# Both halves of the weighted values ahead of the two multiplies that read them, in a fused attention and feed-forward kernel

## The chip, the cores and the metric

The kernel runs on one core of one Trainium2 chip. The metric is the time of one execution on the device in microseconds (us), and the median over several executions is quoted. A profiled execution also gives a span, from the first to the last instruction, which is about 1.8 us shorter than that time; slots and waits below are read in the span. PE is TensorE (PEld its weight loads), DVE is VectorE, ACT is ScalarE, POOL is GpSimd. The granted clock is the share of TensorE's full clock that the profile shows as granted: 1.00 is full, 0.50 half. The chain is the work that ended last, followed back from the last instruction through what each step waited for.

## The reference, cut to what matters

```python
# q, k, v: (8, 12, 448, 64)
scores = q @ k.T / sqrt(64)
e = exp(scores - m)
attn = e / (sum(e) + exp(-m) + 1e-09)      # softmax "off by one"
x = (attn @ v)  -> (3584, 768)
h = x @ w_in                               # 768 x 2048
g = h * tanh(softplus(h))                  # mish
out = g @ w_out                            # 2048 x 768
```

The kernel leaves out the maximum: it computes exp(scores) and divides by sum + 1, as logarithm with bias 1 and exponential with scale -1.

## The kernel before

Four heads make a group; there are 24 groups, three to a batch. The weighted values of a group are two halves of 32 columns per head. Four matmuls lie side by side in the array (one per head), four times over, so 16 matmuls make a half. Each half is written to its own 512 columns of one tile of 2 x 512; such a part is called a bank below:

```python
    def sums(g):
        den = m_pool.tile([128, 512], FP32, tag="m", name="den_ps")
        side_by_side(den, g, lambda c, t: ones[0:P, :])
        rc = work.tile([128, S], FP32, tag="rc", name="rc")
        nc.scalar.activation(out=rc, in_=den[:, 0:S], func=AF.Ln, bias=1.0)
        nc.scalar.activation(out=rc, in_=rc, func=AF.Exp, scale=-1.0)
        rc_t[g] = rc

    def attend(g):
        ...
        av = s_pool.tile([128, 2, 512], FP32, tag="s", name="av_ps")
        ...
        for s in range(2):
            side_by_side(av[:, s], g, lambda c, t: vs[:, c, t, s])
            nc.vector.tensor_mul(x_t[b][:, gi, s, :], av[:, s, 0:S], rc)
```

`s_pool` has three buffers of two banks, and the score tiles use them too: `scores` takes a buffer, two matmuls fill it, and one exponential on ScalarE empties it. `m_pool` has two buffers of one bank. After the first groups, each slot of the program runs like this, with matmuls of the feed-forward part (`after_a`, `after_b`, `after_c`) between the scores of the next two pairs of heads, and with mish work on ScalarE in 14 of the slots:

```python
    def group_slot(u, after_a, after_b, after_c, gates_of=None):
        prepare(2 * u)
        sums(u - 1)
        if gates_of is not None:
            mish(*gates_of)
        attend(u - 1)
        if 2 * u < J:
            scores(2 * u, (0, 1))
        run(after_a)
        ...
        scores(2 * u, (2, 3))
        scores(2 * u + 1, (0,))
        run(after_b)
        ...
        scores(2 * u + 1, (1, 2, 3))
        run(after_c)
```

The softmax here doesn't subtract the row's maximum and nothing guards it: scores larger than these inputs give would overflow.

## Time and profile before

| | before |
|---|---|
| time, median of 3 runs | 470.77 us (469.59 to 471.0) |
| span of the profiled run, granted clock | 467.7 us, 1.00 |
| TensorE busy | 427.6 us, 91% |
| ScalarE busy | 285.3 us, 61% |
| VectorE busy | 139.4 us, 30% |
| TensorE waits for the multiply between the halves | 27.4 us in 24 pieces |

TensorE is the engine to watch, since it is busy nearly all the time and makes most of the chain that ended last. What counts is therefore the time in which it stands still, and what it stands still for. The lines are in the prediction.

### The profile page before, as it was taken

The page shows a single profiled execution, that of the slowest core. Times are in us where ns is not written, and L with a number is a line of the kernel's source. Part 1 is how long each engine was busy: PE and PEld are TensorE (multiplying, and loading weights), DVE is VectorE, ACT ScalarE, POOL GpSimd, SP SyncE. Part 2 cuts the span into 40 slices and gives each one's busy share as a digit, 9 for nine tenths or more (in the row PEclk, how much of TensorE's full clock was granted, in tenths as well). Part 3 has the DMA queues.
Part 4 walks back from the last instruction along what each step waited for, and adds up shares of the span by engine and source line. Part 5 has one row for each costly group of instructions (what it writes and reads, how often), then busy time and mean ns, then how long its engine had stood idle before and what let it go on. Part 6 is the DMA issues. An engine that isn't in the chain of part 4 may idle for free.

```text
span 467.7 us, 8046 instructions
## 1 busy us (share of the span) xinstructions
PE 427.6 (91%) x3424; PEld 215.8 (46%) x3424; DVE 139.4 (30%) x232; ACT 285.3 (61%) x346; POOL 87.0 (19%) x144
## 2 busy tenths in 40 slices
PE   7898987998999999999999999999999999999996
PEld 2334443444544445444445445444445444545563
DVE  1224342442224421344223431244223432110021
ACT  3785588777934977458864769349773679342200
POOL 6454131210122211130112311131021100000000
PEclk9999999999999999999999999999999999999999
DMA  9999996330669326770486435590455301210222
GB/s 197 202 202 204 209 180 158 81 80 24 149 167 203 81 67 146 180 170 1 114 205 156 136 80 125 143 229 0 114 142 152 85 2 34 69 35 0 69 68 67
DMA packets 77700, 55.21 MB, mean 118 GB/s; under 512 B 36576, under 2 KB 74208, under 8 KB 77664
## 3 DMA queue, kind: packets, MB, share of 16 engines
q1 hardware_dynamic: 64288, 44.32, 38.6%
q0 software_dynamic: 13216, 10.19, 14.1%
q8 instruction: 26, 0.43, 0.4%
q10 hardware_dynamic: 160, 0.20, 0.1%
q14 instruction: 10, 0.08, 0.1%
HBM read 45.61 MB, written 11.01 MB: 121 GB/s over the span
## 4 chain that ended last, share of the span: by engine, by line
PE 78%; ACT 13%; DVE 3%; DMA 3%; issue 1%; POOL 1%; DVEq 0%; POOLq 0%
PE o_ps L261 31%; PE h_ps L207 29%; PE s_ps L153 8%; PE av_ps L176 4%; PE den_ps L176 4%; ACT e L160 4%; ACT rc L189 3%; DVE xT L201 3%; ACT rc L188 3%; DMA kq<-in_q_dram 3%; ACT gm L238 2%; ACT L239 1%; ACT L235 1%; PE tr_ps L136 1%; DMA out_dram<-o_sb 0%
## 5 line engine op out<-in xcount | busy, mean ns | idle before, releaser
L160 ACT ACTIVATE e<-s_ps 112x896 bf16<-112x896 f32 x192 | 162.7, 917 | 82.7 <-PE s_ps L153 81.9
L207 PE MATMUL h_ps<-xT,w_in_sb 128*128 128x448 bf16 x768 | 152.5, 353 | 0.0
L261 PE MATMUL o_ps<-w_out_sb,gm 128*128 128x384 bf16 x768 | 131.3, 326 | 0.0
L207 PEld LDWEIGHTS <-w_in_sb 128*128 128x128 bf16 x768 | 72.4, 98 | 74.5 <-issue 10.9
L261 PEld LDWEIGHTS <-gm 128*128 128x128 bf16 x768 | 72.9, 98 | 55.1 <-issue 8.6
L215 DVE COPY h_sb<-h_ps 128x448 f32<-128x448 f32 x112 | 70.0, 625 | 85.8 <-PE h_ps L207 85.8
L279 DVE COPY o_sb<-o_ps 128x384 f32<-128x384 f32 x54 | 30.1, 558 | 150.1 <-PE o_ps L261 136.7
L176 PE MATMUL av_ps<-e,v_b 112*32 112x448 bf16 x768 | 45.3, 353 | 27.4 <-DVE xT L201 27.4
L115 POOL CAST kq<-k_f 112x512 bf16<-112x512 f32 x36 | 22.1, 615 | 201.2 <-DMA k_f<-in_k_dram 139.7
L153 PE MATMUL s_ps<-qk 64*112 64x448 bf16 x384 | 55.5, 373 | 4.0 <-ACT e L160 3.3
L201 DVE TENSOR_TENSOR xT<-av_ps,rc 128x448 bf16<-128x448 f32 x48 | 30.0, 625 | 60.5 <-ACT rc L189 35.5
L188 ACT ACTIVATE rc<-den_ps 128x448 f32<-128x448 f32 x24 | 13.1, 547 | 50.9 <-PE den_ps L176 50.9
L176 PEld LDWEIGHTS <-v_b 112*32 112x32 bf16 x768 | 20.9, 96 | 46.7 <-issue 34.1
L238 ACT ACTIVATE gm<-h_sb 128x1536 bf16<-128x1536 f32 x28 | 39.8, 1467 | 0.0
L153 PEld LDWEIGHTS <-qk 64*112 64x112 bf16 x384 | 20.8, 126 | 36.1 <-issue 29.1
L119 POOL CAST v_b<-v_f 112x512 bf16<-112x512 f32 x36 | 22.1, 614 | 54.3 <-PE av_ps L176 49.5
L176 PE MATMUL den_ps<-e,ones 112*32 112x448 bf16 x384 | 23.3, 355 | 0.4 <-ACT e L160 0.2
L115 POOL CAST kq<-q_f 112x512 bf16<-112x512 f32 x36 | 22.1, 614 | 3.5 <-DMA q_f<-in_q_dram 2.8
L219 ACT ACTIVATE gm<-h_ps 128x384 bf16<-128x384 f32 x16 | 7.9, 491 | 22.6 <-PE h_ps L207 22.6
L261 PE MATMUL o_ps<-w_out_sb,gt 128*128 128x384 bf16 x128 | 21.5, 326 | 0.0
L239 ACT ACT_TABLE_LOAD x14 | 18.0, 1283 | 0.3
L235 ACT ACT_TABLE_LOAD x14 | 18.0, 1283 | 0.2
(29 smaller groups left out, 109.9 us busy)
## 6 DMA issues: line engine op xcount, KB each, us to landing
k_f<-in_k_dram SPq DMA_DIRECT2D x37, 224.0 KB, 3.6
q_f<-in_q_dram SPq DMA_DIRECT2D x37, 224.0 KB, 3.8
v_f<-in_v_dram SPq DMA_DIRECT2D x36, 224.0 KB, 4.0
w_in_sb<-in_moe_w_in_dram POOLq DMA_DIRECT2D x8, 384.0 KB, 12.1
w_out_sb<-in_moe_w_out_dram POOLq DMA_DIRECT2D x4, 768.0 KB, 16.0
out_dram<-o_sb SPq DMA_DIRECT2D x8, 336.0 KB, 3.2
out_dram<-o_sb SPq DMA_DIRECT2D x8, 288.0 KB, 2.8
out_dram<-o_sb SPq DMA_DIRECT2D x8, 240.0 KB, 2.7
```

The lines of the kernel that those rows point to most:

```text
L115: nc.gpsimd.tensor_copy(out=mb[:, i].rearrange("p t h d -> p h t d"), in_=loaded.pop((j, name)).rearrange("p h (t d) -> p h t d", d=D),)
L153: nc.tensor.matmul(sp[0:P, h, 0:S], lhsT=qk[r, 0, t * P : (t + 1) * P], rhs=qk[r, 1, :], start=True, stop=True,)
L160: nc.scalar.activation(out=e_t[j][:, t], in_=sp[0:P, :, 0:S], func=AF.Exp, scale=SCALE)
L176: nc.tensor.matmul(ps[c * 32 : c * 32 + 32, 0:S], lhsT=weights(c, t), rhs=e_t[2 * g + c // 2][:, t, c % 2, :], start=(t == 0), stop=(t == ...
L188: nc.scalar.activation(out=rc, in_=den[:, 0:S], func=AF.Ln, bias=1.0)
L201: nc.vector.tensor_mul(x_t[b][:, gi, s, :], av[:, s, 0:S], rc)
L207: nc.tensor.matmul(hp[:, 0:S], lhsT=w_in_sb[:, dm // 2, dm % 2, ff * 128 : (ff + 1) * 128], rhs=x_t[b][:, dm // 2, dm % 2, :], start=(dm = ...
L215: nc.vector.tensor_copy(out=h_sb[:, ff, :], in_=hp[:, 0:S])
L235: nc.scalar.activation(out=gt[:, f, o : o + TAIL], in_=h_sb[:, f, MAIN:S], func=AF.Mish)
L238: nc.scalar.activation(out=gm[:, f, :], in_=h_sb[:, f, 0:MAIN], func=AF.Mish)
L261: nc.tensor.matmul(op[:, 0:HALF], lhsT=lhs, rhs=w_out_sb[:, ff, n * HALF : (n + 1) * HALF], start=(ff == 0), stop=(ff == FF_T - 1),)
L279: nc.vector.tensor_copy(out=o_sb[:, cols], in_=op[:, 0:HALF])
```

## The change

The intent is that the second half should not wait for the multiply of the first. They share a tile, and in the program's order the write of the second half comes after a read of that tile.

```diff
         for s in range(2):
             side_by_side(av[:, s], g, lambda c, t: vs[:, c, t, s])
+        for s in range(2):
             nc.vector.tensor_mul(x_t[b][:, gi, s, :], av[:, s, 0:S], rc)
```

## The prediction

> **What bounds the kernel now.** I read the page first (busy shares, then the chain that ended last), then the waits of TensorE, then the timeline of one slot, and last, for every slot, when each score tile starts and when the buffer that it reuses comes free.
>
> ```profile
> PE 427.6 (91%) x3424; PEld 215.8 (46%) x3424; DVE 139.4 (30%) x232; ACT 285.3 (61%) x346; POOL 87.0 (19%) x144
> PE 78%; ACT 13%; DVE 3%; DMA 3%; issue 1%; POOL 1%; DVEq 0%; POOLq 0%
> L176 PE MATMUL av_ps<-e,v_b 112*32 112x448 bf16 x768 | 45.3, 353 | 27.4 <-DVE xT L201 27.4
> L239 ACT ACT_TABLE_LOAD x14 | 18.0, 1283 | 0.3
> PE av_ps L176 <- DVE xT L201: 27.4, 24, 1.2
> PE s_ps L153 <- ACT e L160: 3.3, 4, 2.1
> ```
>
> TensorE (PE) bounds it: 91% busy, 78% of the chain. Its one large wait is the one that the change is about: 27.4 us in 24 pieces, one for each group of four heads, up to 1.2 us each. All other waits of TensorE together are about 8 us: 3.3 us for exponentials (second line of waits) and the rest nearly all in the first 17 us. The 13% of ScalarE (ACT) and 3% of VectorE (DVE) in the chain are mostly this detour: sums, logarithm, exponential, multiply, second half. The table load's count tells that 14 of the 24 slots also do mish work on ScalarE; this will matter. Here is one such slot, TensorE's lines first:
>
> ```profile
> 222.96 0.94 PE L176 MATMUL den_ps<-e,ones 112*32 112x448 bf16 x16
> 223.72 0.93 PE L176 MATMUL av_ps<-e,v_b 112*32 112x448 bf16 x16
> 225.81 0.94 PE L176 MATMUL av_ps<-e,v_b 112*32 112x448 bf16 x16 [1.16 <-DVE xT L201]
> 226.68 0.59 PE L153 MATMUL s_ps<-qk 64*112 64x448 bf16 x4
> 227.20 5.37 PE L261 MATMUL o_ps<-w_out_sb,gm 128*128 128x384 bf16 x32
> ...
> 224.53 0.58 ACT L189 ACTIVATE rc<-rc 128x448 f32<-128x448 f32 x1
> 225.12 1.28 ACT L235 ACT_TABLE_LOAD   x1
> 226.41 0.63 ACT L235 ACTIVATE gt<-h_sb 128x512 bf16<-128x512 f32 x1
> 226.95 2.84 ACT L238 ACTIVATE gm<-h_sb 128x1536 bf16<-128x1536 f32 x2
> 229.81 1.28 ACT L239 ACT_TABLE_LOAD   x1
> ...
> 225.13 0.62 DVE L201 TENSOR_TENSOR xT<-av_ps,rc 128x448 bf16<-128x448 f32 x1 [1.51 <-ACT rc L189]
> 226.80 0.62 DVE L201 TENSOR_TENSOR xT<-av_ps,rc 128x448 bf16<-128x448 f32 x1 [1.04 <-PE av_ps L176]
> ```
>
> The first half of the weighted values runs at 223.72. Its multiply needs the reciprocal (ready at 225.11) and ends at 225.75; the second half, into the other bank of the same tile, starts only then, at 225.81. It needs neither. The next lines are the last exponential and the last score tile that end the slack of this slot, and the same two of a slot of another kind (36 us later) and of a third without mish:
>
> ```profile
> 231.92 0.91 ACT L160 ACTIVATE e<-s_ps 112x896 bf16<-112x896 f32 x1
> 232.93 0.35 PE L153 MATMUL s_ps<-qk 64*112 64x448 bf16 x2
> ...
> 268.54 0.91 ACT L160 ACTIVATE e<-s_ps 112x896 bf16<-112x896 f32 x1
> 270.02 0.35 PE L153 MATMUL s_ps<-qk 64*112 64x448 bf16 x2
> ...
> 244.31 0.91 ACT L160 ACTIVATE e<-s_ps 112x896 bf16<-112x896 f32 x1
> 249.30 0.35 PE L153 MATMUL s_ps<-qk 64*112 64x448 bf16 x2
> ```
>
> The score tiles and the weighted values' tile share three buffers. The score tile in the second line reuses the buffer that the exponential in the first line frees: free at 232.83, used at 232.93, a slack of 0.10 us. In the other two kinds it is 0.57 and 4.08 us.
>
> **What the Trainium skill says.** "PSUM — Partial Sum Buffer", in its summary of rules for kernel authors, asks for reads of PSUM during matmuls to go to a different bank, guarded by bank. The two halves are in different banks, so nothing of that kind asks for the wait; it comes from the shared tile. The trace agrees only that the wait exists. "Perfetto Trace Analysis", Matmuls, says that independent matmul groups should rotate through different banks so that an evacuation overlaps the next group; here the evacuation doesn't overlap. "TensorE: Matmul & The Clock Gate", Packing small matmuls, gives starts of about 4 ns apart for packed tiles; the trace has 3 to 4 ns within four matmuls and about 0.19 us from four to four. "ScalarE: Activation LUTs", What ACT_TABLE_LOAD costs, gives 1283 ns and a drain of 1380 ns more; the trace shows 1283 ns, but mish starts 0.01 us after the load, so I count no drain.
>
> **The change part by part.** No instruction is added or removed. The built kernel's lists show two moves: the second half's first matmul no longer waits for VectorE, and the first multiply waits for all 32 matmuls of its tile, the second for nothing.
>
> *Saved on TensorE, per slot.* Start to start, sums to first half is 223.72 - 222.96 = 0.76 us, for the same 16 matmuls and a change of tile. First to second half is 2.09 us. It should become 0.76, so 1.33 us is freed; a little more than the idle 1.16 us, since the pipeline's fill goes too. For 24 slots that is 32 us at most.
>
> *The multiplies.* The second half will start at 224.48 and end at 225.42. The first multiply moves from 225.13 to about 225.46, the second ends at about 226.72 in place of 227.42. All later readers get their data sooner, and VectorE (30% busy) has room.
>
> *What stays of it.* ScalarE's chain in a slot hangs on the end of the sums (223.93), which doesn't move: logarithm, exponential, table load, mish, table load, then exponentials of the slot's first two score tiles, ending at 232.83. So in a mish slot TensorE comes to its fifth score tile 1.33 us earlier, but the buffer doesn't. The slot keeps min(1.33, slack - 0.05), 0.05 being the least distance from exponential to matmul in the trace. By the same two columns for all slots:
> - 6 slots without mish (groups 3, 8, 11, 14, 17, 20), where the exponentials follow their scores at once and move with them, and the last one (23, no scores follow): 7 x 1.33 = 9.3 us.
> - Group 2: its last sums already wait for an exponential, and the second half could start at 37.03 in place of 38.33: 1.3 us.
> - 5 mish slots (9, 12, 15, 18, 21) with slack 0.57 to 0.58: 5 x 0.53 = 2.6 us.
> - 6 mish slots (7, 10, 13, 16, 19, 22) with slack 0.10: 6 x 0.05 = 0.3 us.
> - 3 mish slots (4, 5, 6) where TensorE waits for the exponential already (the 3.3 us above): 0.
> - Groups 0 and 1, before mish begins: ScalarE sets the pace there, idle 1.27 and 1.22 us until the first scores after the second half. In group 0 the halves are 1.75 apart: 1.75 - 0.76 = 1.0 us. In group 1 the scores come 1.9 us earlier, counting the first, so 0.9 us more. Together 1.9 us.
>
> Sum: 9.3 + 1.3 + 2.6 + 0.3 + 1.9 = 15.4 us, so half of the 32. The rest turns into a wait of TensorE for exponentials. 470.8 - 15.4 = 455.4 us, 3.3% faster.
>
> **The rivals.** (a) Everything is kept: 32 us off, 439 us. For it speaks that TensorE's wait is the only large one; against it, the slack of 0.10 us. (b) Little is kept, because something else takes the wait's place in all slots, such as the first multiply, now later, or a DMA: then 465 us or more. Against it: the transposed queries and keys land 11.8 us or more before use from the third batch on, where a DMA brings them (landing subtracted from first use), and no reader stands close behind the multiplies except in group 2, where the projection's last matmuls would come at 39.38 and the second multiply ends at 39.27. (c) TensorE's clock falls as the idle time goes. The granted clock is 1.0 with 91% busy now; I give this little. (d) The ScalarE-bound slots keep a bit more, since exponentials of the slot's second half start earlier and smooth the following sums: these sums aren't bound by them now, so it gives nothing.
>
> **Range and chances.** The per-slot figures repeat to 0.02 us across batches, so the sum errs mostly in the first three groups (3 us) and in the 0.57 class. If the groups at the start give nothing, 458.6; if the 0.57 class keeps everything, 451.4. I take 452.5 to 459.5. Faster by 2% needs 9.4 us, and the slots without mish give that nearly alone: 0.95; within 2% 0.045; slower 0.005.
>
> **What would show it.** The wait of TensorE's second half for the multiply is gone. In its place stands a wait of the scores for exponentials of about 19 us: 3.3 + 3 x 1.33 + 6 x 1.28 + 5 x 0.80 = 19.0. A slot without mish, from sums to sums, is 1.33 us shorter; a slot with slack 0.57 by 0.53; one with slack 0.10 by 0.05. Busy time of each engine stays as it is. I am wrong if the wait for exponentials is under 10 us with a time under 450, if a wait for the multiply or a DMA appears on TensorE, if the second half doesn't follow the first by about 0.76 us, or if the granted clock falls.

## The result, and the profile after

The changed kernel takes 457.48 us (median of 4 runs, 455.26 to 458.42) against 470.88 us (median of 4, beside the same runs). The ratio of the fast runs is 0.9713, with a 95% interval from 0.9671 to 0.9754: 2.9% faster. A ratio here is the mean time of one kernel's fast runs over that of the other's of the same rounds, so it isn't quite the ratio of the medians. All runs of both are of the fast state; single looks below have no state, being one run.

The same rows of the page and of TensorE's waits as before:

```profile
PE 431.6 (95%) x3424; PEld 216.9 (47%) x3424; DVE 136.8 (30%) x232; ACT 284.0 (62%) x346; POOL 87.5 (19%) x144
PE 66%; ACT 28%; DMA 3%; issue 1%; POOL 1%; DVE 1%; DVEq 0%; POOLq 0%
L176 PE MATMUL av_ps<-e,v_b 112*32 112x448 bf16 x768 | 41.1, 354 | 0.0
PE s_ps L153 <- ACT e L160: 14.6, 23, 3.4
```

The 27.4 us of idle time before the weighted values are gone altogether. The wait of the scores (`s_ps`) for exponentials has grown from 3.3 to 14.6 us, with one piece of 3.4 us, and ScalarE's share of the chain from 13% to 28%. The span fell by 11.0 us, from 467.7 to 456.6.

The slot that the prediction showed, group 13, in the changed kernel (start, length, engine, instruction; in brackets the idle time before it and what ended it; TensorE first, then VectorE, then ScalarE):

```profile
219.52 1.69 PE L176 MATMUL av_ps<-e,v_b 112*32 112x448 bf16 x32
226.96 0.40 PE L153 MATMUL s_ps<-qk 64*112 64x448 bf16 x2
227.86 0.40 PE L153 MATMUL s_ps<-qk 64*112 64x448 bf16 x2 [0.51 <-ACT e L160]
228.67 0.40 PE L153 MATMUL s_ps<-qk 64*112 64x448 bf16 x2 [0.41 <-ACT e L160]
...
221.33 1.16 DVE L202 TENSOR_TENSOR xT<-av_ps,rc 128x448 bf16<-128x448 f32 x2 [1.91 <-PE av_ps L176]
...
226.90 2.53 ACT L160 ACTIVATE e<-s_ps 112x896 bf16<-112x896 f32 x3
```

The 32 matmuls run in one piece. The third score tile comes at 226.96, 7.44 us after the first weighted values; before it was 232.50 - 223.72 = 8.78 us, so 1.34 us has been won up to there. The fourth and fifth tiles then wait for the exponentials of this slot's first two tiles, and nearly all of it is lost again: the fifth tile starts 9.15 us after the first weighted values, before 232.93 - 223.72 = 9.21 us.

The start of a slot without mish, group 8:

```profile
131.00 1.69 PE L176 MATMUL av_ps<-e,v_b 112*32 112x448 bf16 x32
132.61 0.58 PE L153 MATMUL s_ps<-qk 64*112 64x448 bf16 x4
138.44 0.78 PE L153 MATMUL s_ps<-qk 64*112 64x448 bf16 x6
```

Here all six matmuls of the third to fifth tile run in one piece, with no wait, and the 1.34 us is kept.

For each group I took the start of its first weighted values, and from that the length of its slot (to the same instruction of the next group). The table has how much shorter than before the slots became, in us, good to 0.01 us since the starts are rounded. Two of the experiments are beside it, since they are the same table:

| groups | predicted | changed kernel | old order in groups 4 to 6 | new order, work moved |
|---|---|---|---|---|
| 0 | 1.0 | 0.49 | 0.77 | 0.76 |
| 1 | 0.9 | 1.33 | 1.33 | 1.33 |
| 2, 3 | 1.3, 1.33 | 1.33, 1.35 | 1.34, 1.34 | 1.33, 1.35 |
| 4, 5, 6 (mish) | 0, 0, 0 | -1.63, -1.68, 0.00 | 0.00, 0.00, 0.00 | -2.52, 0.00, 0.00 |
| 8, 11, 14, 17, 20 | 1.33 each | 1.34 or 1.35 | 1.34 or 1.35 | 1.34 or 1.35 |
| 9, 12, 15, 18, 21 (mish) | 0.53 each | 0.48 or 0.49 | 0.48 | 1.34 or 1.35 |
| 10, 16, 22 (mish) | 0.05 each | 0.00 or 0.01 | 0.01 | 1.34 |
| 7, 13, 19 (mish) | 0.05 each | 0.00 or 0.01 | 0.00 or 0.01 | 0.00 or 0.01 |
| 23, to the end | 1.33 | 1.32 | 1.36 | 1.35 |

The prediction holds slot by slot within 0.05 us from group 2 on, with one exception: groups 4 and 5 did not stay as they were, but became 1.63 and 1.68 us longer. (Groups 0 and 1 are off by 0.5 and 0.4 us, in opposite directions.)

In group 4 the timeline of TensorE shows a wait of 3.44 us, and after it 12 matmuls of the projection that take 4.00 us; the same 12 took 2.44 us in the kernel before, where the wait was 2.10 us (first the changed kernel, then the kernel before):

```profile
64.16 0.40 PE L153 MATMUL s_ps<-qk 64*112 64x448 bf16 x2
68.00 0.40 PE L153 MATMUL s_ps<-qk 64*112 64x448 bf16 x2 [3.44 <-ACT e L160]
68.81 0.48 PE L153 MATMUL s_ps<-qk 64*112 64x448 bf16 x2 [0.41 <-ACT e L160]
69.21 4.00 PE L208 MATMUL h_ps<-xT,w_in_sb 128*128 128x448 bf16 x12
```

```profile
71.86 0.40 PE L153 MATMUL s_ps<-qk 64*112 64x448 bf16 x2 [2.10 <-ACT e L160]
72.67 0.40 PE L153 MATMUL s_ps<-qk 64*112 64x448 bf16 x2 [0.41 <-ACT e L160]
73.00 2.44 PE L207 MATMUL h_ps<-xT,w_in_sb 128*128 128x448 bf16 x12
```

The granted clock tells why. Each line is a stretch of time: from and to, its length, busy time and instructions of each engine (PE, PEld, DVE, ACT, POOL), then the granted clock, the DMA share and GB/s. First the changed kernel, then one stretch of the kernel before, at the same place:

```profile
65.58:68.99 3.41, 0.58 (x4) 0.25 (x3) 0.00 (x0) 3.38 (x5) 1.41 (x3) 1.00 0.46 135
68.99:72.41 3.42, 3.42 (x11) 1.35 (x10) 0.62 (x1) 2.19 (x3) 0.43 (x1) 0.50 0.71 177
82.65:86.06 3.41, 1.84 (x11) 0.67 (x10) 0.71 (x2) 3.40 (x4) 0.00 (x0) 1.00 0.02 5
86.06:89.47 3.41, 3.41 (x11) 1.42 (x10) 0.62 (x1) 1.81 (x3) 0.00 (x0) 0.50 0.82 205
```

```profile
67.88:71.30 3.42, 1.89 (x11) 0.76 (x9) 1.25 (x2) 3.39 (x4) 1.57 (x3) 1.00 0.14 39
```

After a stretch in which TensorE was busy for 0.58 of 3.41 us, its clock is 0.50 for the next 3.42 us; the same follows a stretch with 1.84 us. In the kernel before, the waits of that slot lay apart (1.16, 2.10 and 0.41 us), the emptiest such stretch had 1.89 us of work, and the clock stayed at 1.00 from 13.3 us until the last matmul.

### The profile page after: what moved, and what is told of

The parts are those of the page before. It is cut to its first block, busy times and chain, and to the rows that moved or that the text cites. A ratio compares the mean times of both kernels' runs of the same rounds, so it can differ in the third digit from the quotient of the medians.

```text
span 456.6 us, 8046 instructions
## 1 busy us (share of the span) xinstructions
PE 431.6 (95%) x3424; PEld 216.9 (47%) x3424; DVE 136.8 (30%) x232; ACT 284.0 (62%) x346; POOL 87.5 (19%) x144
## 4 chain that ended last, share of the span: by engine, by line
PE 66%; ACT 28%; DMA 3%; issue 1%; POOL 1%; DVE 1%; DVEq 0%; POOLq 0%
PE o_ps L262 25%; PE h_ps L208 24%; ACT gm L239 8%; PE s_ps L153 7%; ACT e L160 6%; PE den_ps L176 5%; ACT L240 4%; ACT L236 4%; PE av_ps L176 3%; DMA kq<-in_q_dram 2%; ACT gt L236 2%; ACT rc L189 2%; ACT rc L188 2%; PE tr_ps L136 1%; PE spare_ps L170 1%
## 5 line engine op out<-in xcount | busy, mean ns | idle before, releaser
L208 PE MATMUL h_ps<-xT,w_in_sb 128*128 128x448 bf16 x768 | 155.7, 358 | 0.0
L208 PEld LDWEIGHTS <-w_in_sb 128*128 128x128 bf16 x768 | 73.4, 99 | 76.2 <-issue 14.2
L153 PE MATMUL s_ps<-qk 64*112 64x448 bf16 x384 | 60.4, 376 | 16.0 <-ACT e L160 14.6
L202 DVE TENSOR_TENSOR xT<-av_ps,rc 128x448 bf16<-128x448 f32 x48 | 27.7, 619 | 45.3 <-PE av_ps L176 45.3
L176 PE MATMUL av_ps<-e,v_b 112*32 112x448 bf16 x768 | 41.1, 354 | 0.0
L220 ACT ACTIVATE gm<-h_ps 128x384 bf16<-128x384 f32 x16 | 7.9, 491 | 21.2 <-PE h_ps L208 21.2
L240 ACT ACT_TABLE_LOAD x14 | 18.0, 1283 | 0.2
L236 ACT ACT_TABLE_LOAD x14 | 18.0, 1283 | 0.2
```

Source lines behind the costliest of these rows:

```text
L153: nc.tensor.matmul(sp[0:P, h, 0:S], lhsT=qk[r, 0, t * P : (t + 1) * P], rhs=qk[r, 1, :], start=True, stop=True,)
L176: nc.tensor.matmul(ps[c * 32 : c * 32 + 32, 0:S], lhsT=weights(c, t), rhs=e_t[2 * g + c // 2][:, t, c % 2, :], start=(t == 0), stop=(t == ...
L208: nc.tensor.matmul(hp[:, 0:S], lhsT=w_in_sb[:, dm // 2, dm % 2, ff * 128 : (ff + 1) * 128], rhs=x_t[b][:, dm // 2, dm % 2, :], start=(dm = ...
L236: nc.scalar.activation(out=gt[:, f, o : o + TAIL], in_=h_sb[:, f, MAIN:S], func=AF.Mish)
L240: nc.scalar.preload_act_table_set("natural_log_exp_and_others")
```

## The experiments

All runs gave the reference's result. Each part of this list ran beside the kernel before, which took 470.88 us (median of 4 runs) beside the changed kernel, 470.81 (median of 23) beside the next four rows, 470.74 (median of 7) beside the two after them, and 470.49 in a single run beside the last three looks.

| run | time, us | runs | ratio to before, 95% interval |
|---|---|---|---|
| changed kernel | 457.48 | 4 | 0.9713 (0.9671 to 0.9754) |
| old order in groups 4 to 6 | 454.34 | 4 | 0.9654 (0.9591 to 0.9717) |
| new order, spare matmuls | 455.11 | 4 | 0.9659 (0.9598 to 0.9719) |
| old order, two tiles | 457.82 | 4 | 0.9724 (0.9683 to 0.9764) |
| old order, work moved | 470.55 | 20 | 0.9995 (0.9981 to 1.0009) |
| new order, work moved | 448.05 | 4 | 0.9540 (0.9498 to 0.9581) |
| new order, more work moved | 441.88 | 4 | 0.9396 (0.9365 to 0.9427) |
| changed kernel, two more looks | 456.51, 458.06 | 1 each | none |
| spare matmuls, one more look | 451.90 | 1 | none |

**Old order in groups 4 to 6.**

```diff
         for s in range(2):
             side_by_side(av[:, s], g, lambda c, t: vs[:, c, t, s])
+            if g in (4, 5, 6):
+                nc.vector.tensor_mul(x_t[b][:, gi, s, :], av[:, s, 0:S], rc)
         for s in range(2):
-            nc.vector.tensor_mul(x_t[b][:, gi, s, :], av[:, s, 0:S], rc)
+            if g not in (4, 5, 6):
+                nc.vector.tensor_mul(x_t[b][:, gi, s, :], av[:, s, 0:S], rc)
```

> Groups 4, 5 and 6 keep the old order; all others have the new one. My theory: these three slots gain nothing from the new order, and two of them lose 1.64 and 1.68 us because TensorE's idle time, once spread over two waits, gathers into one of 3.4 us and its granted clock halves for a window. With the old order there the clock should stay at 1.0 from 22 us on, slots 4 and 5 take 14.9 and 20.4 us again, and the whole is about 454.3 us (457.5 - 3.3), with less spread between runs. Rival: the clock falls because TensorE is busier as a whole; then the windows of half clock come elsewhere and the time stays at 456.5 to 458.5 us.

Measured: 454.34 us, and in the profiled execution no stretch of half clock from 12.7 us until the last matmuls are done. The three slots are within 0.01 us of the kernel before, and all others gain as in the changed kernel (table above), but for group 0, where the changed kernel's profile still had half clock until 21.2 us. The spread didn't become less: 452.24 to 457.36 us, and one of the unprofiled runs has a granted clock of 0.988, for which there is no trace to tell where it fell. So taking the change back in three slots costs nothing; the slots show the cause, the medians (whose intervals overlap) only agree with it.

**Spare matmuls in the waits of groups 4 to 6, new order.** The spare matmuls write a tile that nobody reads.

```diff
         run(after_a)
+        if 5 <= u <= 7:
+            idle(12 if u == 5 else 5)
```

> The new order, with spare matmuls (12, 5 and 5, about 0.19 us each) where TensorE waits for the exponentials in the slots of groups 4, 5 and 6; the results are the reference's. My theory (idle time halves the clock): no window of half clock after 22 us, about 454.3 us as in the run with the old order in these slots. Rival (a busier TensorE halves the clock): the clock falls at least as much, 457.5 us or more.

Measured: 455.11 us. The three slots are 0.00 to 0.01 us off those of the kernel before, and there is no half clock between 20.0 us and the end of the work. This kernel has *more* matmuls than the changed one and keeps its clock there in both of its profiles (the second is below), so the rival (a busier TensorE is throttled) falls. Two of its unprofiled runs have a granted clock of 0.990, within the changed kernel's 0.983 to 0.992; no trace tells where it fell in them.

**Three more looks,** two of the changed kernel and one of that with the spare matmuls, to see where the half clock falls.

> The changed kernel again, for one more look at where its clock halves. My theory: at least one window of half clock (3.4 us) in or just after the wait of 3.4 us in the slot of group 4, near 68 us, and none in the slots from the third batch on, where no wait exceeds about 0.7 us; a window after the shorter waits of groups 5 and 6 (1.2 us and 0.4 us) in some executions only. Slots 4 and 5 lose what their windows cost, all others are as before within 0.05 us. Rival (a busier core): windows also in the later slots.

> The same again, with the same expectations: a window near 68 us; groups 5 and 6 with or without one.

> The kernel with spare matmuls in those waits again: no window of half clock after 22 us. Rival: a window in the slots of groups 4 to 6 as without the spare matmuls.

Measured: in both looks of the changed kernel the clock halves in the slot of group 4 (from 66.6 us for 6.8 us in one, from 68.3 us for 3.4 us in the other); slot 4 is 2.66 and 1.36 us longer than before. In the first of them groups 5 and 6 are undisturbed; in the second, group 6 loses 1.67 us and group 5 nothing. Later slots have none, as expected. With the spare matmuls there was again none from 12.6 us until the last matmul, and the three slots are within 0.01 us of the kernel before. Its stretches around the wait of group 4, now with matmuls in it:

```profile
63.80:67.20 3.40, 1.95 (x11) 0.93 (x11) 0.00 (x0) 3.39 (x6) 2.38 (x4) 1.00 0.85 235
67.20:70.60 3.40, 3.40 (x27) 1.45 (x29) 1.44 (x3) 2.63 (x5) 1.73 (x4) 1.00 1.06 263
```

The stretches ahead of group 5's and group 6's scores in the second look, and the stretch after:

```profile
81.90:85.30 3.40, 1.83 (x12) 0.70 (x9) 1.15 (x2) 3.37 (x5) 0.00 (x0) 1.00 0.02 5
102.40:105.80 3.40, 1.82 (x11) 0.66 (x10) 0.88 (x2) 3.39 (x4) 0.00 (x0) 1.00 0.00 0
105.80:109.20 3.40, 3.40 (x12) 1.55 (x12) 0.00 (x0) 2.00 (x3) 0.00 (x0) 0.50 0.00 0
```

Both stretches have the same work, 1.83 and 1.82 us of 3.4; only after the second did the clock fall. At about half busy, it goes either way. After the start the half clock comes in pieces of 3.41 us, or two of them, and these pieces lie at other places of the program in each execution, which is why the same kernel loses 3.3, 2.7 or 3.0 us by it (sums of the three profiled executions).

**The old order, with each half in a tile of its own.**

```diff
-        av = s_pool.tile([128, 2, 512], FP32, tag="s", name="av_ps")
+        av = [s_pool.tile([128, 2, 512], FP32, tag="s", name="av_ps") for _ in range(2)]
         ...
         for s in range(2):
-            side_by_side(av[:, s], g, lambda c, t: vs[:, c, t, s])
-            nc.vector.tensor_mul(x_t[b][:, gi, s, :], av[:, s, 0:S], rc)
+            side_by_side(av[s][:, 0], g, lambda c, t: vs[:, c, t, s])
+            nc.vector.tensor_mul(x_t[b][:, gi, s, :], av[s][:, 0, 0:S], rc)
```

> The order of the kernel before (half, multiply, half, multiply), but each half in a tile of its own. My theory: the wait came from the shared tile, and its order in the program matters only through that; TensorE's wait for the multiply is gone, and the time is that of the changed kernel, 455 to 459 us. Rival: the interleaved order itself costs, through the multiply's place in VectorE's queue or the buffers; then the time is near 470.8 us.

Measured: 457.82 us, as the changed kernel. The mish slots from group 7 on save the same 0.48 us or nothing, and group 4 has its half clock here, too (1.17 us longer). From group 2 on, those without mish save 1.06 us, 0.28 less than with one tile. Group 8 shows why:

```profile
128.93 1.69 PE L176 MATMUL av_ps<-e,v_b 112*32 112x448 bf16 x32
130.55 0.87 PE L153 MATMUL s_ps<-qk 64*112 64x448 bf16 x4
130.34 1.16 DVE L201 TENSOR_TENSOR xT<-av_ps,rc 128x448 bf16<-128x448 f32 x2 [1.51 <-ACT rc L189]
```

The first line is the point: the multiplies stand between the halves in the program's order, and TensorE still runs all 32 matmuls in one piece. So it is the shared tile that made the wait, and the order matters only through it. The first multiply starts as soon as the reciprocal is there. The price is a second buffer: the four score matmuls take 0.87 us in place of 0.58, since the second tile's buffer is that of the first half, which a multiply of about 0.6 us frees.

**Work moved inside the slots, in the old order.** From group 9 on, one projection unit (six matmuls) goes ahead of the third score tile in five mish slots (9, 12, 15, 18, 21), and two output units (16 matmuls) in three (10, 16, 22).

```diff
-                group_slot(u + 1, cut(m1, 5), m1, cut(m2, 2), (p - 1, 0))
-                group_slot(u + 2, cut(m2, 4), cut(m2, n // 4 - 1 & ~1), m2, (p - 1, 1))
+                group_slot(u + 1, cut(m1, 6), m1, cut(m2, 2), (p - 1, 0))
+                group_slot(u + 2, cut(m2, 6 if n == 16 else 4), cut(m2, 2), m2, (p - 1, 1))
```

> The kernel before, with work moved inside the mish slots from the third batch on: one projection unit more (1.13 us) ahead of the third score tile in five slots, two output units more (2.66 us) in three, as much less after it. In the kernel before no score tile waits there, so my theory says no change: 470.8 +- 0.7 us. Rival: the move helps by itself, by 3 us or more.

Measured: 470.55 us, ratio 0.9995. Every slot from group 1 on is within 0.01 us of the kernel before. The move alone is worth nothing.

**The same move in the new order.**

> The same move of work as in the run on the kernel before, now with the new order. My theory: TensorE waits there for the exponentials that free the score tiles' buffers, and the moved work fills that wait: five slots gain 0.8 us and three gain 1.3 us more, 7.9 us together, from 457.5 to about 449.6 us; each moved slot from the third batch on is then 1.33 us shorter than before. Rival: the buffers are not what holds the slot, and the time stays at 457 us, as the move did nothing on the kernel before.

Measured: 448.05 us, ratio 0.9540. The five slots with 0.48 us now save 1.34 or 1.35 us, and the three with 0.01 save 1.34 us; the slots that weren't touched are as they were (last column of the table), up to the half clock in group 4. A move that is worth nothing without the change is worth 5 x 0.86 + 3 x 1.33 = 8.3 us with it. So these slots were held by the exponentials that free the score tiles' buffers, as the prediction has it: more work ahead of the third tile lets ScalarE come that far. The median went down by 9.4 us, a little more than this; the spread of the two kernels is 3 us each.

**More work moved, in the first batches too.** Two units go from the slots of groups 2 and 3 to that of group 4. In the slot of group 5, one unit goes ahead of its third score tile, and one leaves for the slot of group 6, which the expectation below doesn't count (matmuls of the projection in the slots of groups 2 to 6: 30, 36, 30, 72, 24 before, 24, 30, 42, 66, 30 in this run).

```diff
+                # (the two lines of the run before this, too)
-                group_slot(u, cut(m1, 1), cut(m1, 2), cut(m1, 2))
+                group_slot(u, cut(m1, 1), cut(m1, 1), cut(m1, 2))
...
-                group_slot(u + 1, cut(m1, 2), cut(m1, 2), cut(m1, 2))
-                group_slot(u + 2, cut(m1, 2), cut(m1, 2), m1, (0, 0))
+                group_slot(u + 1, cut(m1, 1), cut(m1, 2), cut(m1, 2))
+                group_slot(u + 2, cut(m1, 4), cut(m1, 2), m1, (0, 0))
...
-                group_slot(u, cut(m1, 4), cut(m1, 4), cut(m1, 4), (0, 1))
+                group_slot(u, cut(m1, 5), cut(m1, 3), cut(m1, 3), (0, 1))
```

> As the run before this, and also in the first batches: two projection units moved from the two slots without mish to the slot of group 4, ahead of its third score tile, and one in the slot of group 5. My theory: group 4's wait of 3.85 us takes up 2.3 us of work and group 5's wait of 1.57 us takes 1.1 us, so 3.4 us less work elsewhere, and with shorter idle stretches the clock isn't halved in them (3.3 us): about 443.5 us, with 442 to 447 allowing for the clock. Rival: moved work is only shifted; about 449.6 us.

Measured: 441.88 us, ratio 0.9396, the best of all, 6.2 us less than the run before it and just below the range that I gave. Groups 2 and 3 save 2.29 and 2.48 us (0.96 and 1.13 more), group 5 saves 2.27 us where it saved nothing, and group 4 stays at 0.00 where it lost 2.52 us. Group 6 takes in its unit and is no longer than before (0.00), so one unit more than the expectation counted fills a wait; this is the likely reason for the time below the range. From the page and the waits:

```profile
PE 426.4 (97%) x3424; PEld 215.6 (49%) x3424; DVE 136.8 (31%) x232; ACT 285.1 (65%) x346; POOL 87.4 (20%) x144
PE s_ps L153 <- ACT e L160: 5.2, 10, 1.2
```

TensorE is 97% busy, the wait for exponentials is down from 14.6 to 5.2 us, and the profiled execution has no half clock between 16 us and the end of the work.

## Why the prediction was right or wrong

It was right in the time (455.4 predicted, 457.48 measured, inside 452.5 to 459.5) and in what carries it; one of its steps failed.

- *The wait between the halves goes, and a slot is freed of 1.33 us.* Right: 1.32 to 1.36 us in all slots that keep it, and 0.0 us of idle time before the weighted values. The trace's idle time (1.16 us) would have been too small a figure, start to start was the right one.
- *Half of it is kept, since the fourth and fifth score tiles wait for exponentials in the mish slots.* Right, and shown by the pair of runs with moved work. The class sizes: 0.53 predicted, 0.48 or 0.49 measured; 0.05 predicted, 0.00 or 0.01 measured. Where the clock was undisturbed, in the run with the old order in groups 4 to 6, the slots' savings add up to 15.3 us (15.4 predicted for the changed kernel).
- *Groups 0 and 1 give 1.9 us.* Together 1.82 us in the changed kernel's profile, 2.1 us in runs whose clock wasn't halved there; only the split between the two was off. What comes before the first weighted values varies between executions by more than that, from 1.2 us later to 2.3 us earlier than in the profile before, and the change has no part in it. The six profiles with a piece of half clock between 14 and 22 us reach them 0.3 us before to 1.2 us after the profile before, the other four 0.8 to 2.3 us before it; so part of the spread of each kernel's runs may come from there, which no experiment tested.
- *The three slots that are bound already give nothing, and the clock gets little weight.* This failed: they gave -1.63, -1.68 and 0.00 us. One of the prediction's own signs of being wrong came true, "if the granted clock falls": it was 1.00 in the profile before and 0.983 in the profile after. With it TensorE's busy time, which was to stay, rose from 427.6 to 431.6 us. Rival (c) named the granted clock, but by "the idle time goes", and the runs show the opposite: what halves it is that the idle time, spread over three waits before, gathers into one in group 4 (3.44 us, 3.2 us with two tiles, with half clock after it in all five profiles that have it), and into 1.16 and 0.41 us close together in groups 5 and 6. That cost 3.3 us in the profiled execution. It is the larger part of the gap in span: 15.4 predicted, 11.0 measured; the rest is 0.63 us at the start and small differences either way.
- *A wait of 19 us for exponentials.* Measured 14.6 us, in the right slots. I had counted starts that are put off, but the row counts idle time, and at each stall the matmul before is still running for a part of it. In group 13 the fifth tile is put off by 1.28 us, and the two idle pieces are 0.51 + 0.41 = 0.92 us. With 0.92 in six slots, 0.41 in five, and 3.85, 1.57 and 1.58 in groups 4 to 6, the sum is 14.6.
- *Rivals (a), (b) and (d).* All kept: no, only in the slots that aren't bound, or once work is moved. Another wait in all slots: no; after the first two groups TensorE waits for no multiply and no DMA. A bit more in the bound slots: no.
- *A reading of the chain.* Of ScalarE's 13% and VectorE's 3% only about half is the detour, not most: by the page's lines the reciprocal's two instructions and the multiply have 3% each, and the rest goes mainly to score exponentials and mish. Nothing in the sum rests on it.

## What to carry to other kernels

Before counting a wait as gain, ask in each slot which wait comes next and how far away it is: here a slack of 0.10, 0.57 or over 4 us decided the gain of each slot, and it could be read off the trace beforehand. Once the first wait is gone, a move of work that was worth nothing before can be worth more than half of the change again, so look at the schedule anew. And where idle time is moved rather than removed, look at how it gathers, for here one stretch of 3.44 us on TensorE halved its clock where 1.16, 2.10 and 0.41 us apart did not.

## What the Trainium skill lacked or had wrong

- "TensorE: Matmul & The Clock Gate", What's actually happening and HAM oscillation: it puts the fall of the clock at an idle window or gap of about 3.4 us (its later section on a second failure mode says that short idle pieces can do it too, but not how many). The length of the pieces agrees (3.41 us), but far less idle time is enough: stretches of that length with TensorE busy for 1.84 and 1.82 us, where the longest gap was about 1.2 us, were each followed by half clock. Adding up busy time in every such stretch, from 22 us to the last projection, in all eleven profiled executions: a busy share of 0.05 to 0.19 halved the clock in all five cases, 0.51 to 0.59 in two of eight, and 0.60 and more never, as long as the clock was full.
- "ScalarE: Activation LUTs", What ACT_TABLE_LOAD costs: its 1283 ns are what the traces show, but not the drain of about 1380 ns more. In group 13 of the kernel before, the reciprocal ends at 225.11, the load runs from 225.12 to 226.40, and the next activation starts at 226.41.
- No page has it: the idle time that a trace shows before a stalled matmul is less than what the stall costs, because the matmuls before it are still running: 16 of them take 0.93 us here, but the next 16 start after 0.76 us where nothing holds them. 1.16 us shown were 1.33 to 1.35 us of the slot.
